# Agent attention and a gated feed-forward on one core: query scores moved one group ahead, score products summed in one PSUM bank

## The chip, the core and the metric

The kernel runs on one core of a Trainium2 chip. The core has a matrix engine (TensorE, PE in the profile; its weight loads are PEld), a vector engine (VectorE, DVE), a scalar engine for activation functions and copies (ScalarE, ACT), GpSimd (POOL) and SyncE (SP), whose queue issues most of the transfers. Each engine works through its own instructions in order and waits for others by semaphores. Matmuls read SBUF and write PSUM; a PSUM tile of this kernel is one bank, 512 float32 per partition.

The metric is the device time of one launch in microseconds; less is better. The kernel before takes 2173.52 us, the median of 3 runs (2172.88 to 2175.33).

## The reference

Four batches of 12480 rows of 128, 49 agents, and a feed-forward of width 2048:

```python
def sm(a, b):
    s = scale * (a @ b.transpose(0, 2, 1))
    s = s - s.max(-1, keepdims=True)
    e = np.exp(s)
    return e / (e.sum(-1, keepdims=True) + 1e-09)
agent_v = sm(agents, k) @ v          # per batch, 49 x 128
x = sm(q, agents) @ agent_v          # per batch, 12480 x 128
h = x @ w_in                         # 49920 x 2048
out = (h * (1.0 / (1.0 + np.exp(-1.702 * h)))) @ w_out
```

The scale is 1/sqrt(128). The weights of the feed-forward come as float64; everything else is float32. q, k and agents are multiplied by 8 after drawing.

## The kernel before

**Layout.** Everything runs transposed, with features on partitions. A group is 960 rows of one batch (`GT`), two halves of 480 (`CH`); a batch has 13 groups, the whole has 52. The hidden width is 16 blocks of 128 (`NF`), so a group has 16 steps and the kernel 832, taken two at a time by `two_steps` (L704): 416 pairs of steps.

**Folded weights.** `agent_v @ w_in` is computed once per batch (`weights_part`, L330, four parts of 512 columns), so that a group's hidden values come from the softmax of the 49 agents instead of from x. Precision is kept by splitting operands into a high half (float32r, a rounded form) and a low half, the rest. For the up matmuls the 49 agent rows and their halves are packed into two tiles `wh` and `wq`, and for each group the softmax is packed into `sa`, `sb` and `rq` (`query_pairs`, L383 to L404): TensorE transposes the softmax (L387), ScalarE casts two high parts (L397), VectorE subtracts the low parts (L399), and eight small transfers on SP's queue (`move`, L345) put rows into their places, the last of them into `rq`.

**A pair of steps.** `up` (L408) runs four matmuls with `sa` or `sb` (L415) and four small ones with `rq` on quarters of the array (L418), into four PSUM tiles, which is all that pool has; four gelus on ScalarE follow (L428). `high` (L431) makes the high half of each gelu tile: by a GpSimd transfer that casts (even steps, L434), on ScalarE (L436, steps 1, 3, 5, 11, 13, 15) or on VectorE (L438, steps 7 and 9). `low` (L441) subtracts on VectorE. `down` (L447) runs six matmuls per step (high by high, low by high, high by low, two halves each) and adds 16 steps up in the two `po` tiles; it works four steps behind (`LAG`). In each pair VectorE takes the low half of the even step two back, and of the odd step just made. TensorE takes the odd step of two first, then the jobs of the second step, then the even one.

**Work beside it.** Lists of jobs per step (`at`, filled by `put`) place the rest by hand. Per group, for the next one: score halves at steps 2 and 3 (`Q_AT`), the shift by the maximum at step 4, exp at 6 (`E_AT`; ScalarE loads another function table for it and then the gelu table again), sums at 8, softmax at 9, transposes and packing at 10 (`P_AT`); for the one after it, the splitting of the loaded queries into three bfloat16 parts at 13 to 16 (`S_AT`, `split`). Per batch, for the next one: 13 key tiles, one each 5 or 6 steps (split, two score halves, partial maximum), the key maximum, then 13 value tiles, two a group (L288), then the four weight parts. `pe_step` keeps TensorE's extra jobs on separate steps.

**Scores.** `scores` (L178) sums six products of bfloat16 parts in four matmuls per block of 120 rows: parts 0 and 1 of the agents side by side (98 columns), part 2 (49 columns), and so on. Each half (four blocks) fills one PSUM tile with two column sets per block; ScalarE copies one set (L193), and VectorE adds the other (L194). The partial maximum of a key tile is a reduction over 8 blocks (L229).

**Order.** The Tile framework sets all semaphores and orders the part ahead of the loop and the first group by its own scheduler; from the second group on the order on TensorE, ScalarE, VectorE and GpSimd is as written (`manual_schedule`, L732). Ahead of the loop lie the loads, the first batch's key scores and values, four conversions of float64 words for `w_in` (`to_float32`, L116, eight VectorE operations), query 0, the four weight parts of batch 0, and one of the four conversions for `w_out`.

Of the kernel before, what the change touches and what calls it, by code (L numbers as in the profile page):

```python
# [42 lines left out]
def kernel(  # L43
# [62 lines left out]
    part_max = const.tile([P, NKG, A], F32, name="part_max")  # L106
# [71 lines left out]
    def scores(b, parts, out, c):  # L178
        x0, x1, x2 = parts
        a = ag_part[:, b].rearrange("p i a -> p (i a)")  # L180
        mm = nc.tensor.matmul
        ps = ps_m.tile([P, 512], F32, name="ps_m")
        for j in range(KB // 2):
            t0 = (c * KB // 2 + j) * TB
            t = slice(t0, t0 + P)
            o = ps[:, j * 2 * A : (j + 1) * 2 * A]
            mm(out=o, lhsT=x0[:, t], rhs=a[:, 0 : 2 * A], start=True, stop=False)  # L187
            mm(out=o[:, A:], lhsT=x0[:, t], rhs=a[:, 2 * A :], start=False, stop=False)
            mm(out=o, lhsT=x1[:, t], rhs=a[:, 0 : 2 * A], start=False, stop=False)  # L189
            mm(out=o[:, 0:A], lhsT=x2[:, t], rhs=a[:, 0:A], start=False, stop=True)  # L190
        s = ps[:TB, : KB * A].rearrange("p (j i a) -> p j i a", i=2, a=A)
        o = out[:, c * KB // 2 : (c + 1) * KB // 2, :]
        nc.scalar.copy(out=o, in_=s[:, :, 0, :])  # L193
        return lambda: nc.vector.tensor_add(out=o, in0=s[:, :, 1, :], in1=o)  # L194
# [7 lines left out]
    def first_key_scores(g, kt):  # L202

        for c in range(2):
# [12 lines left out]
        nc.vector.tensor_reduce(  # L217
            out=part_max[:TB, g, :],
            in_=score[:TB, g * KB : (g + 1) * KB, :].rearrange("p j a -> p a j"),
            axis=AX.X,  # L220
            op=ALU.max,
        )

    def key_scores(b, g, parts, c):
        return scores(b, parts, score[:TB, g * KB : (g + 1) * KB, :], c)

    def key_part_max(g):
        s = score[:TB, g * KB : (g + 1) * KB, :]
        nc.vector.tensor_reduce(  # L229
            out=part_max[:TB, g, :], in_=s.rearrange("p j a -> p a j"), axis=AX.X, op=ALU.max  # L230
        )
# [98 lines left out]
    def weights_part(b, w, c):  # L330
# [23 lines left out]
    def query_scores(n, b, parts, c):  # L354
        sd = e_sb[:TB, :, 0:A]
        return sd, scores(b, parts, sd, c)

    def query_shift(sd):
        m = work.tile([P, KB], F32, name="m")
        nc.vector.tensor_reduce(out=m[:TB], in_=sd, axis=AX.X, op=ALU.max)  # L360
# [70 lines left out]
    def high(f, g):  # L431
        gh = gpool.tile([P, 2, CH], F32R, name="gh", bufs=GH_BUFS)
        if f % 2 == 0:
            nc.gpsimd.dma_start(out=gh, in_=g)  # L434
        elif f in HI_ON_ACT:
            nc.scalar.copy(out=gh, in_=g)  # L436
        else:
            nc.vector.tensor_copy(out=gh, in_=g)  # L438
# [7 lines left out]

    def down(f, gh, gl, po):  # L447
        for lhsT, rhs, first, last in (
# [4 lines left out]
            for c in range(2):  # L453
# [4 lines left out]
                    start=(f == 1 and first),  # L458
                    stop=(f == NF - 2 and last),
# [17 lines left out]
    adds = {}  # L477
# [28 lines left out]
    def do_key_scores(b, g, c):  # L506
        adds[b, g, c] = key_scores(b, g, k_parts[b, g], c)
# [9 lines left out]
    def do_query_scores(n, c):  # L517
        if n < B * NG:
            b, g = divmod(n, NG)
            scored[n], adds[n, c] = query_scores(n, b, q_parts[n], c)  # L520

    def do_query_add(n, c):
        if n < B * NG:
            adds.pop((n, c))()
# [35 lines left out]
    for g in range(NKG):  # L560
# [13 lines left out]
    for c in range(2):  # L574
        do_query_scores(0, c)
        do_query_add(0, c)
    do_query_shift(0)
    do_query_exp(0)
    do_query_sums(0)
    do_query_softmax(0)  # L580
    acc_ps = ps_o.tile([P, 512], F32, name="po0")
    for g in range(NKG):
# [11 lines left out]
        if g in FIRST_UP:  # L594
            up_weights(FIRST_UP.index(g), words_in[FIRST_UP.index(g)])
# [6 lines left out]
    do_query_load(1)  # L602
# [23 lines left out]
    for i in range(1, NF // 4):  # L626
# [147 lines left out]
```

## Time and profile before

| | |
|---|---|
| median of 3 runs | 2173.52 us (2172.88 to 2175.33) |
| the profiled execution | 2182.02 us, span 2180.2 us |
| mean granted TensorE clock | 0.968 |
| busy: PE, DVE, ACT, POOL | 94%, 76%, 67%, 13% of the span |
| first pair of steps | at 78.8 us |
| DMA | 349.46 MB, mean 160 GB/s |

Busy shares are averages over the span. A busy TensorE may run at a lower clock, and matmuls are pipelined, so the distance from one start to the next says what a matmul costs, not its duration. In the lines shown below, an idle time and what ended it stand in brackets or behind the bar. The clock is in parts of full speed.

### The profile page before, as it was taken

How to read it: one execution, taken by the hardware profiler on the slowest of the kernel's cores; microseconds unless marked ns; L12 is line 12 of the kernel's file. 1: busy time of each engine (PE TensorE's matmuls, PEld its weight loads, DVE VectorE, ACT ScalarE, POOL GpSimd, SP SyncE). 2: the span in 40 equal slices, each digit the busy share in tenths (PEclk: the TensorE clock that was granted, in tenths of full speed). 3: DMA queues.
4: the chain of work that ended last, by engine and by line, in shares of the span. 5: the costliest groups of instructions: out<-in, count | busy, mean ns of one | idle time of the engine just before them, and what ended most of it. 6: DMA issues, size and time to landing. Idle time of an engine off the chain costs nothing.

```text
span 2180.2 us, 33873 instructions
## 1 busy us (share of the span) xinstructions
PE 2055.0 (94%) x12232; PEld 1562.0 (72%) x12232; DVE 1659.4 (76%) x2220; ACT 1471.6 (67%) x2602; POOL 287.2 (13%) x577
## 2 busy tenths in 40 slices
PE   7899999999999999999999999999998999999999
PEld 7567776777767777767776777777776777777776
DVE  6699887777779888777777989787676666766665
ACT  3367676676767776676676676666776776767775
POOL 3011111111101111111101111111110111111110
PEclk9799999999999999999999999999999999999999
DMA  9455566686545546777644545776754444443433
GB/s 266 126 175 174 168 161 170 161 188 171 162 134 164 178 153 170 176 179 172 177 145 140 178 153 167 184 168 170 186 137 137 142 136 141 136 142 133 135 133 122
DMA packets 162460, 349.46 MB, mean 160 GB/s; under 512 B 17900, under 2 KB 88332, under 8 KB 162292
## 3 DMA queue, kind: packets, MB, share of 16 engines
q0 software_dynamic: 100464, 223.68, 36.1%
q1 hardware_dynamic: 61828, 123.61, 19.7%
q8 instruction: 96, 1.57, 0.3%
q14 instruction: 72, 0.59, 0.1%
HBM read 100.14 MB, written 25.56 MB: 58 GB/s over the span
## 4 chain that ended last, share of the span: by engine, by line
PE 46%; DMA 17%; issue 10%; DVE 7%; ACT 3%; SPq 3%; POOL 1%; POOLq 0%; ACTq 0%; DVEq 0%
PE po L454 27%; DMA rq<-sb 11%; PE ph L415 8%; PE ph L418 5%; DMA gh<-g 4%; SPq L346 3%; DVE gl L443 3%; ACT g L428 2%; DMA wq<-wl 2%; PE ps_m L290 1%; PE ps_m L187 1%; PE ps_m L387 1%; DVE gh L438 1%; PE ps_m L189 1%; POOL gh L434 1%
## 5 line engine op out<-in xcount | busy, mean ns | idle before, releaser
L428 ACT ACTIVATE g<-ph 128x480 f32<-128x480 f32 x1664 | 821.9, 576 | 596.6 <-PE ph L418 586.6
L443 DVE TENSOR_TENSOR gl<-g,gh 128x960 fp32r<-128x960 f32 x832 | 950.5, 1152 | 241.2 <-DMA gh<-g 122.8
L454 PE MATMUL po<-gh,wo_h 128*128 128x480 f32 x1664 | 564.2, 421 | 0.0
L454 PE MATMUL po<-gl,wo_h 128*128 128x480 f32 x1664 | 512.9, 390 | 0.0
L454 PE MATMUL po<-gh,wo_l 128*128 128x480 f32 x1664 | 510.9, 389 | 0.0
L434 POOL DMA_DIRECT2D gh<-g x416 | 222.5, 535 | 1802.0 <-ACT g L428 1409.5
L454 PEld LDWEIGHTS po<-gl,wo_h 128*128 128x128 f32 x1664 | 322.6, 194 | 53.8 <-issue 0.8
L454 PEld LDWEIGHTS po<-gh,wo_l 128*128 128x128 f32 x1664 | 321.9, 194 | 53.6
L454 PEld LDWEIGHTS po<-gh,wo_h 128*128 128x128 f32 x1664 | 281.5, 194 | 84.9 <-issue 63.5
L415 PE MATMUL ph<-sb,wh 128*128 128x480 f32 x832 | 318.0, 382 | 7.4 <-DMA sb<-sb 7.4
L415 PE MATMUL ph<-sa,wh 128*128 128x480 f32 x832 | 319.2, 384 | 0.5 <-DMA wh<-wl 0.4
L436 ACT CAST gh<-g 128x960 fp32r<-128x960 f32 x312 | 314.3, 1007 | 6.9
L418 PE MATMUL ph<-rq,wq 19*128 19x480 f32 x1664 | 249.4, 483 | 51.2 <-DMA rq<-sb 42.4
L418 PEld LDWEIGHTS ph<-rq,wq 19*128 19x128 f32 x1664 | 97.4, 182 | 216.3 <-issue 140.4
L415 PEld LDWEIGHTS ph<-sb,wh 128*128 128x128 f32 x832 | 157.9, 190 | 35.9 <-issue 9.2
L415 PEld LDWEIGHTS ph<-sa,wh 128*128 128x128 f32 x832 | 158.2, 190 | 28.9 <-issue 2.0
L174 DVE TENSOR_TENSOR rest<-rest 128x488 bf16<-128x488 f32 (+1 forms) x182 | 128.7, 715 | 0.0
L189 PE MATMUL ps_m<-ag_part,rest 128*128 128x98 bf16 x728 | 115.3, 205 | 0.0
L190 PE MATMUL ps_m<-ag_part,rest 128*128 128x49 bf16 x728 | 111.9, 186 | 0.0
L194 DVE TENSOR_TENSOR e_sb<-ps_m,e_sb 120x196 f32<-120x196 f32 x104 | 37.1, 357 | 88.4 <-ACT e_sb L193 88.4
L438 DVE CAST gh<-g 128x960 fp32r<-128x960 f32 x104 | 68.2, 656 | 34.7 <-ACT g L428 34.6
L399 DVE TENSOR_TENSOR sa<-ps_m,sa 49x480 fp32r<-49x480 f32 x52 | 33.9, 651 | 58.9 <-ACT sb L397 54.9
(103 smaller groups left out, 1798.0 us busy)
## 6 DMA issues: line engine op xcount, KB each, us to landing
gh<-g POOLq DMA_DIRECT2D x416, 480.0 KB, 3.8
kt<-kT SPq DMA_DIRECT2D x52, 480.0 KB
qt<-qT SPq DMA_DIRECT2D x52, 480.0 KB
vt<-v SPq DMA_DIRECT2D x52, 480.0 KB
outT<-o SPq DMA_DIRECT2D x104, 240.0 KB
v_pair<-v POOLq DMA_DIRECT2D x39, 480.0 KB, 7.1
rq<-sa SPq DMA_DIRECT2D x104, 35.6 KB
rq<-sb SPq DMA_DIRECT2D x104, 35.6 KB
```

What stands on the lines that cost most here:

```text
L174: nc.vector.tensor_sub(out=halves(r)[1][:, s], in0=r[:, s], in1=halves(r)[0][:, s])
L189: mm(out=o, lhsT=x1[:, t], rhs=a[:, 0 : 2 * A], start=False, stop=False)
L190: mm(out=o[:, 0:A], lhsT=x2[:, t], rhs=a[:, 0:A], start=False, stop=True)
L346: nc.sync.dma_start(out=out.bitcast(F32), in_=in_.bitcast(F32))
L415: nc.tensor.matmul(out=ph[k][:, :CH], lhsT=wh[:, cols[i]], rhs=pairs[c], start=True, stop=False)
L418: nc.tensor.matmul(out=ph[k][:, :CH], lhsT=wq[r, cols[i]], rhs=rq[r], start=False, stop=True, tile_position=(k * 32, 0),)
L428: nc.scalar.activation(out=gs[i][:, c, :], in_=ph[k][:, :CH], func=AF.Gelu_apprx_sigmoid)
L434: nc.gpsimd.dma_start(out=gh, in_=g)
L436: nc.scalar.copy(out=gh, in_=g)
L438: nc.vector.tensor_copy(out=gh, in_=g)
L443: nc.vector.tensor_sub(out=gl, in0=g, in1=gh.bitcast(F32))
L454: nc.tensor.matmul(out=po[c][:, :CH], lhsT=lhsT[:, f, :], rhs=rhs[:, c, :], start=(f == 1 and first), stop=(f == NF - 2 and last),)
```

## The change

- The query work of a group is done two groups ahead up to the shift, and one group ahead from the exp on: splits at steps 8 to 11, score halves at 12 and 13, load and shift at 14, exp at step 0 of the next group, sums and softmax at 2, transposes and packing at 4. Queries 0 and 1 are taken up to the softmax ahead of the loop (`ahead`).
- `scores` runs six matmuls of 49 columns per block, all summed in the same 49 columns; both halves of a tile share one PSUM bank (`score_bank`). ScalarE's copy and VectorE's add of a half go: the query's maximum and shift read the bank, and a key tile is copied once, as a whole (`key_store`).
- The key maximum is kept as a running elementwise maximum over tiles (`running_max`), read from the same bank, and reduced over the 8 blocks at the end.
- High halves: step 1 goes to a GpSimd transfer too, step 3 to VectorE, the other odd steps to ScalarE. Both low halves of a pair are taken in the next pair, the odd one first; that of step 1 one pair later still. The first down matmuls of a group take step 0 first.
- The high half of a value tile is a VectorE copy of the loaded tile in place of a GpSimd transfer. Value matmuls move to steps 6 and 11 of a group (the last tile: 5), key tiles to one each 5.5 steps in batches 1 and 2.
- Ahead of the loop only one `w_in` conversion precedes the value loads; the loads of words alternate between `w_in` and `w_out`. Two weight parts are made ahead of the loop, two in the first group, with their conversions. The first `wq` moves go to GpSimd's queue. The written order holds from the first group on.

```diff
-Q_AT = 2
-E_AT = 6
-P_AT = 10
-S_AT = 13
+Q_AT = 12
+E_AT = 0
+P_AT = 4
+S_AT = 8
 K_AT = 3
-V_AT = 0
-V2_AT = 9
+V_AT = (6, 11)
+V_LAST = 5
-FIRST_WORDS = (1, 3, 5, 7)
-FIRST_UP = (0, 2, 4, 6)
-HI_ON_ACT = (1, 3, 5, 11, 13, 15)
+FIRST_WORDS = 1
+FIRST_UP = 2
+BOTH = (0,)
+ON_DVE = (2,)
...
-    def scores(b, parts, out, c):
+    def scores(b, parts, ps, c):
         x0, x1, x2 = parts
...
+        for j in range(c * KB // 2, (c + 1) * KB // 2):
+            t = slice(j * TB, j * TB + P)
+            o = ps[:, j * A : (j + 1) * A]
+            products = [(x0, 0), (x0, 1), (x0, 2), (x1, 0), (x1, 1), (x2, 0)]
+            for i, (x, y) in enumerate(products):
+                nc.tensor.matmul(
+                    out=o,
+                    lhsT=x[:, t],
+                    rhs=ag_part[:, b, y, :],
+                    start=(i == 0),
+                    stop=(i == len(products) - 1),
+                )
+
+    def score_bank():
         ps = ps_m.tile([P, 512], F32, name="ps_m")
...
+        return ps, ps[:TB, : KB * A].rearrange("p (j a) -> p j a", a=A)
...
+    def running_max(g, s):
+        if g == 0:
+            nc.vector.tensor_copy(out=run_max[:TB], in_=s)
+        else:
+            nc.vector.tensor_tensor(out=run_max[:TB], in0=s, in1=run_max[:TB], op=ALU.max)
+
+    def key_store(g, s):
+        nc.scalar.copy(out=score[:TB, g * KB : (g + 1) * KB, :], in_=s)
+        running_max(g, s)
...
-    def value_hi(b, g):
-        nc.gpsimd.dma_start(out=v_pair[:TB, :, 0:C], in_=v[b, :, g * KB : (g + 1) * KB, :])
-
-    def value_lo(g, vt):
+    def value_pair(vt):
         vp = v_pair
+        nc.vector.tensor_copy(out=vp[:TB, :, 0:C], in_=vt[:TB])
         nc.vector.tensor_sub(out=vp[:TB, :, C : 2 * C], in0=vt[:TB], in1=vp[:TB, :, 0:C].bitcast(F32))
...
-        if f % 2 == 0:
+        if f % 2 == 0 or f - 1 in BOTH:
             nc.gpsimd.dma_start(out=gh, in_=g)
-        elif f in HI_ON_ACT:
+        elif f - 1 in ON_DVE:
+            nc.vector.tensor_copy(out=gh, in_=g)
+        else:
             nc.scalar.copy(out=gh, in_=g)
...
+    def ahead(n):
+        for c in range(2):
+            do_query_scores(n, c)
+        do_query_load(n + 1)
+        do_query_shift(n)
+        do_query_exp(n)
+        do_query_sums(n)
+
+    ahead(0)
     do_query_softmax(0)
...
-    for c in range(F // 512):
+    for c in range(2):
+        if c:
+            up_weights(c, words_in[c])
         weights_part(0, w0, c)
+    for i in range(4):
+        do_query_split(1, i)
+    ahead(1)
+    do_query_softmax(1)
     down_weights(0, words[0])
...
     for i in range(1, NF // 4):
+        if i > 1:
+            put(4 * i - 8, lambda i=i: up_weights(i, words_in[i]))
+            put(pe_step(4 * i - 6), lambda i=i: weights_part(0, w0, i))
         put(4 * i - 3, lambda i=i: down_weights(i, words[i]))
...
-            t = pe_step(s0 + (10 + 5 * k if b == 0 else K_AT + 6 * k))
+            t = pe_step(s0 + (16 + 5 * k if b == 0 else K_AT + 11 * k // 2))
             t1 = pe_step(t + 1)
...
-            put(t1 + 1, lambda b=b, k=k: adds.pop((b + 1, k, 1))())
-            put(t1 + 1, lambda k=k: key_part_max(k))
+            put(t1 + 1, lambda b=b, k=k: do_key_store(b + 1, k))
...
+            t = slot + (V_LAST if last else V_AT[k % 2])
...
+            put(t - 4, lambda b=b, k=k: value_pair(vts.pop((b + 1, k))))
+            put(slot + 3 - last, lambda k=k: key_pair(k))
...
+        if n:
+            put(s0 + E_AT, lambda n=n: do_query_exp(n + 1))
...
+            put(s0 + E_AT + 2, lambda n=n: do_query_sums(n + 1))
+            put(s0 + E_AT + 2, lambda n=n: do_query_softmax(n + 1))
         put(s0 + P_AT, lambda n=n: do_query_pairs(n + 1))
         for i in range(4):
...
+            put(s0 + S_AT + i, lambda n=n, i=i: do_query_split(n + 2, i))
+        for c in range(2):
+            put(s0 + Q_AT + c, lambda n=n, c=c: do_query_scores(n + 2, c))
+        put(s0 + Q_AT + 2, lambda n=n: do_query_load(n + 3))
+        put(s0 + Q_AT + 2, lambda n=n: do_query_shift(n + 2))
...
+        for u in late:
+            do_low(u)
+        late.clear()
         jobs(t)
         if t < steps:
             gh[t] = high(f, g[t])
+            if f not in ON_DVE:
+                gh[t + 1] = high(f + 1, g[t + 1])
         if 2 <= t < steps + 2:
-            gl[t - 2] = low(g.pop(t - 2), gh[t - 2])
-        if t < steps:
+            if (f - 2) % NF in BOTH:
+                late.append(t - 1)
+            else:
+                do_low(t - 1)
+        downs = []
+        if t >= LAG:
+            m, e = divmod(t - LAG, NF)
...
+            downs = [0, 1] if e in BOTH else [1, 0]
+        for k, i in enumerate(downs):
+            u = t - LAG + i
+            down(e + i, gh.pop(u), gl.pop(u), po[m], e + k == 0, e + k == NF - 1)
+            if k == 0:
+                second(t, f)
...
+    def second(t, f):
+        jobs(t + 1)
+        if 2 <= t < steps + 2:
+            do_low(t - 2)
+        if t < steps and f in ON_DVE:
             gh[t + 1] = high(f + 1, g[t + 1])
...
     with tc.manual_schedule(engines={E.PE, E.Activation, E.DVE, E.Pool}):
-        for t in range(NF, steps + LAG, 2):
+        for t in range(0, steps + LAG, 2):
             two_steps(t)
```

More of the change, by code (lines that the diff above doesn't have):

```diff
@@ L105 @@
     score = const.tile([P, NKG * KB, A], F32, name="score")
-    part_max = const.tile([P, NKG, A], F32, name="part_max")
+    run_max = const.tile([P, KB, A], F32, name="run_max")
     max_b = const.tile([P, A], F32, name="max_b")
@@ L216, in first_key_scores @@
             nc.scalar.copy(out=score[:TB, i * KB // 2 : (i + 1) * KB // 2, :], in_=s)
[L217 to L231, printed above, removed]
+        running_max(g, score[:TB, g * KB : (g + 1) * KB, :])
+    def running_max(g, s):
[6 more added lines that the diff above has]
+        running_max(g, s)
     def key_max_0(d):
         mx = work.tile([P, A], F32, name="mx", bufs=1)
-        nc.vector.tensor_reduce(
-            out=mx[:TB], in_=part_max[:TB].rearrange("p g a -> p a g"), axis=AX.X, op=ALU.max
-        )
+        nc.vector.tensor_reduce(out=mx[:TB], in_=run_max[:TB].rearrange("p j a -> p a j"), axis=AX.X, op=ALU.max)
         d["mx"] = mx
@@ L342, in weights_part, with move @@
         for i in range(4):
-            move(wq[i * 32 : i * 32 + A - R, s], wl[R:A])
-    def move(out, in_):
-        nc.sync.dma_start(out=out.bitcast(F32), in_=in_.bitcast(F32))
+            move(wq[i * 32 : i * 32 + A - R, s], wl[R:A], None if b or c else nc.gpsimd)
+    def move(out, in_, queue=None):
+        (queue or nc.sync).dma_start(out=out.bitcast(F32), in_=in_.bitcast(F32))
     def query_load(b, g):
@@ L352, in query_load, with query_shift @@
         return t
-    def query_scores(n, b, parts, c):
+    def query_shift(s):
+        m = work.tile([P, KB], F32, name="m")
+        nc.vector.tensor_reduce(out=m[:TB], in_=s, axis=AX.X, op=ALU.max)
         sd = e_sb[:TB, :, 0:A]
[L356 to L360, printed above, removed]
         nc.vector.tensor_tensor(
-            out=sd, in0=sd, in1=m[:TB].unsqueeze(2).broadcast_to([TB, KB, A]), op=ALU.subtract
+            out=sd, in0=s, in1=m[:TB].unsqueeze(2).broadcast_to([TB, KB, A]), op=ALU.subtract
         )
+        return sd
     def query_exp(e):
@@ L444, in low, with down @@
         return gl
-    def down(f, gh, gl, po):
+    def down(f, gh, gl, po, begin, end):
         for lhsT, rhs, first, last in (
@@ L457, in down @@
                     rhs=rhs[:, c, :],
-                    start=(f == 1 and first),
-                    stop=(f == NF - 2 and last),
+                    start=(begin and first),
+                    stop=(end and last),
                 )
@@ L476 @@
     scored = {}
-    adds = {}
+    banks = {}
     sums = {}
@@ L506, in do_key_scores, with do_key_store @@
     def do_key_scores(b, g, c):
-        adds[b, g, c] = key_scores(b, g, k_parts[b, g], c)
+        if c == 0:
+            banks[b, g] = score_bank()
+        scores(b, k_parts[b, g], banks[b, g][0], c)
+    def do_key_store(b, g):
+        key_store(g, banks.pop((b, g))[1])
     def do_key_values(b, g):
@@ L518, in do_query_scores @@
         if n < B * NG:
[L519 to L524, printed above, removed]
+            if c == 0:
+                banks[n] = score_bank()
+            scores(n // NG, q_parts[n], banks[n][0], c)
     def do_query_shift(n):
         if n < B * NG:
-            query_shift(scored[n])
+            scored[n] = query_shift(banks.pop(n)[1])
     def do_query_exp(n):
@@ L565 @@
         nc.sync.dma_start(out=vt0[:TB, g % 2, :, 0:C], in_=v[0, :, g * KB : (g + 1) * KB, :])
-        if g in FIRST_WORDS:
-            words_in.append(load_words(w_in, len(words_in)))
-    words = [load_words(w_out, i) for i in range(NF // 4)]
+        if g == FIRST_WORDS:
+            words_in.append(load_words(w_in, 0))
+    words = []
+    for i in range(NF // 4):
+        if i:
+            words_in.append(load_words(w_in, i))
+        words.append(load_words(w_out, i))
     for g in range(NKG):
@@ L573 @@
     key_max()
[L574 to L579, printed above, removed]
+    def ahead(n):
[6 more added lines that the diff above has]
+    ahead(0)
     do_query_softmax(0)
@@ L626 @@
     for i in range(1, NF // 4):
+        if i > 1:
+            put(4 * i - 8, lambda i=i: up_weights(i, words_in[i]))
+            put(pe_step(4 * i - 6), lambda i=i: weights_part(0, w0, i))
         put(4 * i - 3, lambda i=i: down_weights(i, words[i]))
-    for i in range(4):
-        put(0, lambda i=i: do_query_split(1, i))
     exps = {}
@@ L702, in jobs @@
             job()
+    late = []
     def two_steps(t):
```

72 lines of the change are left out of this document (17 added, 55 removed).

## The prediction

> **What bounds the kernel now.** I read the page's busy shares, then the lines of the pair's first matmul, then TensorE's timeline around the start of a group, then who waits, then the granted clock by stretch.
>
> ```profile
> PE 2055.0 (94%) x12232; PEld 1562.0 (72%) x12232; DVE 1659.4 (76%) x2220; ACT 1471.6 (67%) x2602; POOL 287.2 (13%) x577
> ```
> ```profile
> L415 PE MATMUL ph<-sa,wh x832: 374/380/769, 78.8 to 2167.1; 128*128 128x480 f32 x167
> ```
> ```profile
> 1004.90 0.38 PE L415 MATMUL ph<-sa,wh 128*128 128x480 f32 x1
> ...
> 1009.01 0.38 PE L415 MATMUL ph<-sa,wh 128*128 128x480 f32 x1
> ...
> 1012.03 1.20 PE L290 MATMUL ps_m<-v_pair,e_pair 120*128 120x258 f32 x8
> ...
> 1014.37 0.39 PE L415 MATMUL ph<-sa,wh 128*128 128x480 f32 x1
> ```
>
> TensorE (PE) sets the time, but its 94% includes waiting. L415 runs `sa` twice in a pair of steps, so 832 matmuls are 416 pairs, and the last pair starts at 2167.1 - 0.4 = 2166.7. A pair that waits for nothing takes 1009.01 - 1004.90 = 4.11 us (4.10 below); the average is (2166.7 - 78.8)/415 = 5.03. A value tile adds 5.36 - 4.10 = 1.26. Now the first pair of a group, and the score tile in the pair after it:
>
> ```profile
> 1872.19 0.38 PE L415 MATMUL ph<-sa,wh 128*128 128x480 f32 x1
> ...
> 1874.91 0.48 PE L418 MATMUL ph<-rq,wq 19*128 19x480 f32 x1 [0.95 <-DMA rq<-sb]
> ...
> 1878.04 0.38 PE L415 MATMUL ph<-sa,wh 128*128 128x480 f32 x1
> ...
> 1879.43 0.22 PE L187 MATMUL ps_m<-ag_part,qt 128*128 128x98 bf16 x1
> 1879.49 0.19 PE L188 MATMUL ps_m<-ag_part,qt 128*128 128x49 bf16 x1
> 1879.52 0.20 PE L189 MATMUL ps_m<-ag_part,rest 128*128 128x98 bf16 x1
> 1879.56 0.19 PE L190 MATMUL ps_m<-ag_part,rest 128*128 128x49 bf16 x1
> ...
> 1880.01 0.46 PE L454 MATMUL po<-gh,wo_h 128*128 128x480 f32 x1
> ```
> ```profile
>   DMA rq<-sb: 110.7, 123
> ```
> ```profile
> 1860.93 0.60 PE ps_m L387 x4
> ...
> 1868.66 6.21 DMA rq<-sb
> ```
> ```profile
> 1833.90:1837.30 3.40, 2.47 (x11) 1.39 (x9) 3.35 (x4) 2.19 (x4) 0.26 (x1) 1.00 0.48 165
> 1837.40:1840.80 3.40, 3.40 (x9) 2.86 (x10) 2.23 (x2) 1.57 (x2) 0.17 (x1) 0.53 0.41 147
> ```
>
> That first pair took 5.85 us: its last L418 matmul waited for the transfer `rq<-sb`. The chain says why: transposed at 1860.93 (step 10 of the group before), the pieces are moved in one queue, and the last transfer lands 6.21 us after its issue, at 1874.87, 14 us in all, where step 10 leaves six steps, or 12.3 us. This wait sums to 110.7 us over 123 waits (list for tile `rq`). The windows' rows give length, busy time of PE, PEld, DVE, ACT and POOL, granted clock, DMA share and GB/s: one group's first pair left TensorE idle for 0.93 of 3.40 us, and in the next 3.40 us the clock stood at 0.53. Some stalls are paid again in slow matmuls.
>
> In clean terms the stretch from 78.8 to 2166.7 is 415 x 4.10 = 1702; 90 score tiles of two halves, 1880.01 - 1879.43 = 0.58 each, 1.2 with the switch: 108; 39 value tiles: 49; 51 transposes at about 0.5: 26; weight parts 12, from 24 of these 32 matmuls:
>
> ```profile
> L336 PE MATMUL ps_m<-w_in_sb,avT 128*128 128x512 f32 x32 | 18.9, 689 | 2.6 <-DVE avT L324 2.4 <-DVE wl L339 0.2
> ```
>
> That is 1897 of 2088. TensorE loses 191 us, 111 of it directly to `rq`.
>
> **The change, part by part.** *Queries ahead.* Transposes and moves go from step 10 to step 4: twelve steps, 24.6 us at least, for the chain of 14. SP's queue carries the same eight moves, now ahead of the loads of the later steps and behind the stores of step 2; the first weight parts' `wq` moves go to GpSimd's queue, which is idle then. The `rq` stall goes from every group but the first. What is late next is the Vector engine's low half of step 3, as below.
>
> *Scores.* Four matmuls per block (98, 49, 98, 49 columns) become six of 49. The rows give 0.06 and 0.04 after a 98-column matmul and 0.03 after a 49-column one; 16 in 0.58 us are 36 ns on average, about 43 and 27, each with its own weight load. Six at 27 are 162 ns against 140: +0.18 us a tile. Bounds: 24 ns each would make it +0.03, 43 ns (a load that does not keep up) +0.94. I take 27, since 49-column matmuls with weight loads are in the rows. The Trainium skill (TensorE: Matmul & The Clock Gate, Back-to-back issue gap) speaks against the change: a stream of weight load and matmul pairs sustains about 81 ns even at 128 columns; by it, as an estimate, 16 more a tile cost 1.3 us, 115 us in all. The trace disagrees: 36 ns on average, and the measurement decides.
>
> *Vector and Scalar work.*
>
> ```profile
> L193 ACT COPY e_sb<-ps_m 120x196 f32<-120x196 f32 x104 | 37.3, 358 | 10.1 <-PE ps_m L190 10.1
> L194 DVE TENSOR_TENSOR e_sb<-ps_m,e_sb 120x196 f32<-120x196 f32 x104 | 37.1, 357 | 88.4 <-ACT e_sb L193 88.4
> L194 DVE TENSOR_TENSOR score<-ps_m,score 120x196 f32<-120x196 f32 x78 | 28.0, 359 | 5.8 <-ACT score L193 5.2
> L229 DVE TENSOR_REDUCE part_max<-score 120x49 f32<-120x392 f32 x39 | 33.2, 851 | 1.3
> L269 DVE TENSOR_TENSOR score<-score,max_b 120x392 f32<-120x392 f32 x40 | 23.1, 578 | 0.0
> L438 DVE CAST gh<-g 128x960 fp32r<-128x960 f32 x104 | 68.2, 656 | 34.7 <-ACT g L428 34.6
> ```
>
> Vector loses both adds (37 + 28), half of L438's casts (34), and 39 x (0.851 - 0.578) = 11 by the running maximum at L269's price; it gains the values' high half, 1024 columns at about L438's 0.66 to 0.7, 39 times: 27. Net -83, to 1576 us, 76% of the new span; Scalar loses about 40. Neither is the bound over a group. Their order is: these engines work in order, and Vector work waiting for Scalar holds the low halves behind it, which TensorE's down matmuls need. Three places:
>
> (1) Step 0, exp. Two table loads and an exp now follow the group's first pair.
>
> ```profile
> 1854.52 1.28 ACT L366 ACT_TABLE_LOAD   x1
> 1855.81 0.53 ACT L366 ACTIVATE e_sb<-e_sb 120x392 f32<-120x392 f32 x1
> 1856.36 1.28 ACT L428 ACT_TABLE_LOAD   x1
> 1857.65 1.96 ACT L428 ACTIVATE g<-ph 128x480 f32<-128x480 f32 x4
> ```
>
> A pair's gelus end 1.39 + 0.1 + 1.96 = 3.45 after its start (1.39, the up matmuls, is 1879.43 - 1878.04), so the exp ends at 3.45 + 1.28 + 0.53 = 5.3 and gelu resumes 1857.65 - 1854.52 = 3.13 later, at 6.6. The next pair's gelus then end at 8.5, and its successor (8.2) wants its fourth PSUM tile at 8.9: no stall. A key exp of two tiles adds 0.7 (twice the columns of the 0.53 row, in one instruction): at most 0.4. On Vector the sums and softmax follow the exp, 1.3 at L269's price, then with keys four pair copies, 1.9 less some overlap; the value pair fits into the gap ahead of the exp. `low` of step 0 (1.15, half of the 2.23 row below) then ends at 7.8, with keys at 9.7, for a down matmul at 8.2 + 1.39 + 0.5 = 10.1: hidden by 0.4 to 2.3.
>
> (2) Step 4, the pairs.
>
> ```profile
> 1859.27 0.38 PE L415 MATMUL ph<-sa,wh 128*128 128x480 f32 x1
> ...
> 1863.99 0.38 PE L415 MATMUL ph<-sa,wh 128*128 128x480 f32 x1
> ```
> ```profile
> 1863.75 0.65 DVE L399 TENSOR_TENSOR sa<-ps_m,sa 49x480 fp32r<-49x480 f32 x1 [1.90 <-ACT sb L397]
> 1864.43 0.66 DVE L399 TENSOR_TENSOR sb<-ps_m,sb 49x480 fp32r<-49x480 f32 x1
> 1865.12 2.23 DVE L443 TENSOR_TENSOR gl<-g,gh 128x960 fp32r<-128x960 f32 x2
> ```
>
> Vector's subtractions wait behind Scalar's gelus and casts; the first `low` after them ends at 1865.12 + 1.15 = 1866.27. In the changed order the next pair's first down matmul, at 1863.99 + 1.39 = 1865.38, needs just that `low` (step 3): 0.95 us stall, in groups without values. In value groups the key-value matmuls (1.26) stand ahead of it at step 6 and hide it; I leave 0.3.
>
> (3) Key tiles. The maximum now reads the PSUM bank in the same step as Scalar's copy of it. The 1863.75 row shows such a reader waiting for the other engine's last read of its bank: `sa`'s subtraction needs the `sa` cast and waits for `sb`'s. On an even step the copy comes after the pair's matmuls and four gelus (1.39 + 1.96) and takes about 0.5 (0.36 for half of it at L193), so it ends at 4.0, the maximum at 4.5, two split pieces 1.2, `low` 1.1: 5.7 to 6.9, for a down matmul at 4.10 + 1.39 = 5.5. That is 0.2 to 1.4 for about half the stores and something like it when it cascades: 1.9 us a group of three.
>
> *High halves and lag.* Step 1 goes to a GpSimd transfer as well, and every `low` is now taken a pair after its high half. `low` of odd steps no longer waits for its cast; nothing is charged. Each g buffer is held longer, and with five of them gelu stalls about when TensorE would anyway. The value transfers on GpSimd's queue go.
>
> *Start.*
>
> ```profile
> 78.80:126.10 47.30, 43.54 (x194) 27.19 (x195) 34.83 (x57) 28.58 (x49) 4.43 (x11) 0.78 0.42 135
> 126.10:173.10 47.00, 43.77 (x335) 33.66 (x334) 43.14 (x64) 31.05 (x59) 5.23 (x13) 0.96 0.51 165
> ```
> ```profile
> 65.07 0.43 DVE L124 TENSOR_SCALAR tmp<-words 128x512 uint32<-128x512 uint32 x1 [3.34 <-DMA words<-w_out]
> ...
> 68.07 0.28 DVE L600 COPY acc<-po 49x128 f32<-49x128 f32 x1
> ...
> 68.35 0.67 DVE L136 SCALAR_TENSOR_TENSOR m<-m,tmp 128x512 f32<-128x512 f32 x1
> ```
>
> The first two groups took 94 us, at clocks of 0.78 and 0.96. The accumulator copy waited at 68.07 behind a conversion; two weight parts instead of four precede the loop, but query 1's scores and softmax (5 us of Vector work) come in. First pair at 77 (70 to 84). In group 0 Vector has five conversions (two up, three down), 68.35 + 0.67 - 65.07 = 3.9 with the copies in between, 3.6 each, 18; 16 lows at 1.1, 17.6; the rest about 8: 43 against TensorE's 36: 7 lost, and 2 in group 1.
>
> *Sum.* 77 + 416 x 4.10 (1706) + 89 score tiles at 1.38 (123) + values 49 + transposes 26 + weights 14 + tail after the last pair 2180.2 - 2166.7 - 4.1 = 9.4: 2004. Stalls: start 9; 18.5 plain groups at 0.95: 18; 19.5 value groups: 6; 13 key groups: 25; batch changes 3: 61. Slow clock: before, 191 less 111 and some 50 of other waits leaves about 30, 0.2 a stalled microsecond: 12. (The Trainium skill, TensorE: Matmul & The Clock Gate, What's actually happening, has the clock fall only after an idle window of about 3.4 us; by it the short stalls here would cost no clock, and the time would be 12 less. The trace disagrees: TensorE was busy 2.47 of the 3.40 us before the 0.53.) Together 2077 of span, 2079 for the profiled run (2182.02 against its span 2180.2). The median of the runs is 2173.52, 0.996 of the profiled one: **2071**.
>
> **Rivals.** *Vector's waits reach TensorE.* Price a wait on Scalar by L194's, 88.4/39 = 2.3 us. Three per group, exp, pairs and key stores or value pairs, 6.8 us, would be 347 over 51 groups if all reached the down matmuls: 2004 + 9 + 347 of span, 2353 by the median. It is slower than before once half of it arrives (2186 - 2013 = 173). Against it: the Vector engine's slack of 4.1 - 2.2 a pair, and that it waits like this now (88.4 at L194 alone) with little stall from it. Slower: 0.07. A quarter to 40% arriving, 87 to 139 in place of the 61 + 12, gives 2094 to 2145: 0.18.
>
> *Scores at 43 ns:* a weight load that does not keep up with six small matmuls, 89 x 0.76 = +68, 2138: 0.04. For it speaks only that six such in a row, into one region, are not in the trace. (The skill's rule on weight load and matmul pairs points this way.)
>
> *`rq` still late:* were the moves held in SP's queue behind loads, the stall would stay and the scores add 16: with the steadier start about 2175, the same: 0.03.
>
> *All hidden:* no stall but the start's, 2004 + 9 + 2, 2007 by the median, up to 2040: 0.10.
>
> **How the numbers follow.** The forecast, 2045 to 2095, has 0.58. The range 2030 to 2130 leaves out most of the hidden case, the 43 ns case and the slower one. A measurement of this kernel tells about 0.2% (4 us) from no change: faster 0.90, same 0.03, slower 0.07.
>
> **What would show it.** `rq` gone from TensorE's waits; the first pair of a group at 4.1 to 4.3; 48 score matmuls per tile 27 ns apart; no wait of Vector on a score copy in the query's path, but waits on Scalar at the key maximum; the pair after step 4 at about 5.0 in groups without values; clock near 0.99. It is wrong if plain groups take over 37 us (35.6 forecast: 32.8 + 1.38 + 0.5 + 0.95), or if down matmuls wait for `gl` by more than 2 us a group.

## The result and the profile after

The changed kernel takes 2052.34 us (median of 4, 2051.60 to 2052.63); beside it on the same chip the kernel before took 2174.43. The ratio is 0.9429 (95%: 0.9399 to 0.9458): 122 us less, where 102 were forecast. The profiled execution took 2051.6 us with a span of 2049.8, 27 less than the 2077 of the sum.

First the page's busy shares, then the up matmul's line (its first start and its last), then what TensorE's matmuls, its weight loads (PEld) and Vector waited for (us in total, times, longest):

```profile
PE 1998.1 (97%) x13688; PEld 1522.0 (74%) x13688; DVE 1575.9 (77%) x2025; ACT 1443.7 (70%) x2457; POOL 280.1 (14%) x594
```
```profile
L407 PE MATMUL ph<-sa,wh x832: 372/381/769, 77.0 to 2036.5; 128*128 128x480 f32 x167
```
```profile
PE po L445 <- DVE gl L435: 14.3, 17, 5.0
PE ph L410 <- DMA wq<-wl: 6.7, 7, 2.2
```
```profile
PEld po L445 <- DVE gl L435: 36.3, 59, 5.4
PEld ph L407 <- ACT g L420: 21.1, 69, 2.8
```
```profile
DVE sa L391 <- ACT sb L389: 81.8, 42, 7.2
DVE run_max L225 <- ACT score L228: 81.2, 33, 6.9
```

`rq` is gone from TensorE's waits, where it stood with 110.7 us. TensorE executes 1456 more instructions and is busy for 57 us less. Vector's busy time came out as summed: 1575.9 against 1576. Vector waits for Scalar at these two lines for 163 us in all; before, the waits at the score add and at `sa` came to 88.4 + 54.9 = 143.3. The down matmuls and their weight loads wait for low halves (`gl`) for 14.3 + 36.3 = 50.6 us, about 1 us a group. The first pair starts at 77.0. From the starts of L407's rows, the first pairs of all groups together fell from 378.8 to 219.8 us (52 of them), a plain group takes 35.3 us, and a clean pair still takes 4.10. The mean granted clock is 0.988, up from 0.968.

The fourth pair of a plain group stalls, by these rows of a late group's timeline (start, duration, engine, line, operation; the wait before it in brackets):

```profile
1773.88 0.65 DVE L391 TENSOR_TENSOR sa<-ps_m,sa 49x480 fp32r<-49x480 f32 x1 [2.38 <-ACT sb L389]
1773.90 0.38 PE L407 MATMUL ph<-sa,wh 128*128 128x480 f32 x1
...
1774.56 0.66 DVE L391 TENSOR_TENSOR sb<-ps_m,sb 49x480 fp32r<-49x480 f32 x1
...
1775.25 4.36 DVE L435 TENSOR_TENSOR gl<-g,gh 128x960 fp32r<-128x960 f32 x4
...
1776.47 0.71 PE L445 MATMUL po<-gl,wo_h 128*128 128x480 f32 x2 [0.47 <-DVE gl L435]
...
1778.77 0.38 PE L407 MATMUL ph<-sa,wh 128*128 128x480 f32 x1
```

The pair takes 1778.77 - 1773.90 = 4.87 us: Vector idles 2.38 us for Scalar's casts, subtracts twice, and only then makes the low half for which the down matmul waits.

In a group with value tiles another pair stalls too, the third: it takes 5.07 us in most of these 18 groups, against 4.47 in a plain one. Scalar's rows at the start of one:

```profile
1401.37 1.28 ACT L358 ACT_TABLE_LOAD   x1
...
1403.10 0.84 ACT L269 ACTIVATE score<-score 120x784 f32<-120x784 f32 x1
...
1405.25 1.96 ACT L420 ACTIVATE g<-ph 128x480 f32<-128x480 f32 x4
```

The exp of two key tiles (L269) stands beside the query's exp, gelu stands still for 1405.25 - 1401.37 = 3.88 us, and three up matmuls of the third pair wait for a gelu to free their PSUM tile. That is most of the 21.1 us in the list above.

The half score tile of the next step, between its first matmul and the down matmul behind it:

```profile
1788.37 0.25 PE L186 MATMUL ps_m<-ag_part,qt 128*128 128x49 bf16 x3
...
1789.00 0.68 PE L445 MATMUL po<-gh,wo_h 128*128 128x480 f32 x2
```

24 matmuls in 0.63 us are 26 ns each. The Trainium skill (TensorE: Matmul & The Clock Gate, Back-to-back issue gap) has about 81 ns for a sustained pair of weight load and matmul at 128 columns, and an issue floor of about 25 ns for one matmul of up to 64 columns. The trace agrees with the second, though each of these matmuls has its own weight load. A whole tile costs 5.43 - 4.10 = 1.33 us.

Two groups stand out, the first (51.8 us) and the fourteenth, the first of the second batch (52.7 us where its like take 39). The first, as the view of windows has it (length; busy PE, PEld, DVE, ACT, POOL; granted clock; DMA share; GB/s):

```profile
76.98:128.81 51.83, 42.22 (x192) 27.92 (x193) 46.07 (x74) 26.67 (x47) 5.06 (x11) 0.77 0.51 164
```

### The profile page after: what moved, and what is told of

Its sections match the earlier page's. It is cut to its first block, busy times and chain, and to the rows that moved or that the text cites. A ratio compares the mean times of both kernels' runs of the same rounds, so it can differ in the third digit from the quotient of the medians.

```text
span 2049.8 us, 36357 instructions
## 1 busy us (share of the span) xinstructions
PE 1998.1 (97%) x13688; PEld 1522.0 (74%) x13688; DVE 1575.9 (77%) x2025; ACT 1443.7 (70%) x2457; POOL 280.1 (14%) x594
## 4 chain that ended last, share of the span: by engine, by line
PE 78%; DVE 8%; DMA 4%; issue 4%; ACT 4%; SPq 1%; POOL 1%; ACTq 0%; DVEq 0%; POOLq 0%
PE po L445 46%; PE ph L407 15%; PE ph L410 7%; PE ps_m L186 5%; DVE gl L435 4%; ACT g L420 2%; DMA wq<-wl 2%; PE ps_m L284 2%; PE ps_m L209 1%; DVE sb L391 1%; SPq L340 1%; DMA outT<-o 1%; DVE rest L175 1%; DVE rest L173 1%; POOL score L265 1%
## 5 line engine op out<-in xcount | busy, mean ns | idle before, releaser
L445 PE MATMUL po<-gh,wo_h 128*128 128x480 f32 x1664 | 551.2, 412 | 0.0
L445 PE MATMUL po<-gl,wo_h 128*128 128x480 f32 x1664 | 504.1, 384 | 16.1 <-DVE gl L435 14.3
L445 PE MATMUL po<-gh,wo_l 128*128 128x480 f32 x1664 | 499.9, 382 | 0.0
L426 POOL DMA_DIRECT2D gh<-g x468 | 250.1, 534 | 1702.8 <-ACT g L420 1154.6
L445 PEld LDWEIGHTS po<-gl,wo_h 128*128 128x128 f32 x1664 | 309.0, 189 | 82.9 <-DVE gl L435 36.3
L407 PE MATMUL ph<-sa,wh 128*128 128x480 f32 x832 | 320.3, 385 | 4.1 <-DMA wh<-wl 2.2
L407 PE MATMUL ph<-sb,wh 128*128 128x480 f32 x832 | 322.1, 387 | 0.0
L410 PE MATMUL ph<-rq,wq 19*128 19x480 f32 x1664 | 208.9, 483 | 6.7 <-DMA wq<-wl 6.7
L410 PEld LDWEIGHTS ph<-rq,wq 19*128 19x128 f32 x1664 | 81.4, 182 | 145.9 <-issue 136.6
L407 PEld LDWEIGHTS ph<-sa,wh 128*128 128x128 f32 x832 | 157.6, 189 | 36.9 <-ACT g L420 9.6
L407 PEld LDWEIGHTS ph<-sb,wh 128*128 128x128 f32 x832 | 157.5, 189 | 35.4 <-ACT g L420 11.5
L186 PE MATMUL ps_m<-ag_part,rest 128*128 128x49 bf16 x2184 | 128.2, 185 | 0.0
L186 PEld LDWEIGHTS <-rest 128*128 128x128 bf16 x2184 | 108.6, 97 | 0.1
L225 DVE TENSOR_TENSOR run_max<-ps_m,run_max 120x392 f32<-120x392 f32 x36 | 20.4, 566 | 81.3 <-ACT score L228 81.2
L186 PEld LDWEIGHTS <-qt 128*128 128x128 bf16 x1248 | 61.7, 98 | 25.5 <-issue 25.4
```

Of the source, the lines that this page charges most:

```text
L186: nc.tensor.matmul(out=o, lhsT=x[:, t], rhs=ag_part[:, b, y, :], start=(i == 0), stop=(i == len(products) - 1),)
L407: nc.tensor.matmul(out=ph[k][:, :CH], lhsT=wh[:, cols[i]], rhs=pairs[c], start=True, stop=False)
L410: nc.tensor.matmul(out=ph[k][:, :CH], lhsT=wq[r, cols[i]], rhs=rq[r], start=False, stop=True, tile_position=(k * 32, 0),)
L445: nc.tensor.matmul(out=po[c][:, :CH], lhsT=lhsT[:, f, :], rhs=rhs[:, c, :], start=(begin and first), stop=(end and last),)
```

## The experiments

The theory: the gain is the lead of the queries, since the 14 us from the transposes to the landed `rq` now have room. The rival: the gain is the lighter Vector and Scalar work and its order. Times are medians; ratios are to the kernel before on the same chip.

**The packing put back to step 10.**

```diff
-P_AT = 4
-S_AT = 8
+P_AT = 10
+S_AT = 5
```

> The changed kernel with the transposes and packing put back to step 10 of the group before use (splits at 5 so that the written order fits); everything else stays changed. Theory, the lead: the chain from transposes to the landed rq takes 14 us and six steps are 12.3 us, so rq is late again at nearly every group; the direct waits were 111 us before and some 20 us of slow clock came with them: 2150 to 2185 us, first pair of a group at 5.5 to 7.5 us, rq back in TensorE's waits with some 100 us. Rival, the lighter Vector and Scalar engines (score bank, running maximum, order of the halves) brought the gain: 2047 to 2060 us, no rq in the waits.

Measured 2097.9 us, ratio 0.9635 (0.9611 to 0.966): 46 us over the changed kernel, between the two ranges: less than expected but far from none. One group's transposes and the next group's first pair, and the list of waits:

```profile
1824.27 0.63 PE L379 MATMUL ps_m<-ident,p_pad 120*128 120x120 f32 x4
```
```profile
1837.02 0.38 PE L407 MATMUL ph<-sa,wh 128*128 128x480 f32 x1
...
1839.13 0.47 PE L410 MATMUL ph<-rq,wq 19*128 19x480 f32 x1 [0.66 <-DMA rq<-sb]
...
1842.25 0.39 PE L407 MATMUL ph<-sa,wh 128*128 128x480 f32 x1
```
```profile
PE ph L410 <- DMA rq<-sb: 18.0, 22, 1.9
```

`rq` is late again, and the first pair takes 5.23 us. The first pairs of 51 groups take 266.3 us in place of 215.6: 51 us more, a little over the whole difference. The size was off because the lead is not the same six steps as before: now the scores stand in it, at 12 and 13, so that 1837.02 - 1824.27 = 12.75 us pass from the transposes to the group, where before it was 1872.19 - 1860.93 = 11.26. The lead theory stands; the expectation forgot what lies inside the lead.

**The packing at step 8.** The same edit with `P_AT = 8`.

> The same with the transposes at step 8 (splits at 5 too): eight steps are 16.4 us. Theory, the lead with a threshold at 14 us: no wait for rq, 2046 to 2058 us, as with step 4 within 0.3%. If instead each step of lead brought a share of the gain (queues that are only shifted), a third of the way from step 4 to 10 would be lost here twice over: 2090 to 2140 us.

Measured 2108.66 us, ratio 0.9687 (0.9661 to 0.9712). A miss. `rq` was in time:

```profile
PE po L445 <- DVE gl L435: 52.5, 50, 5.0
...
PE ph L410 <- DMA rq<-sb: 3.7, 2, 2.2
```
```profile
1830.76 0.65 DVE L391 TENSOR_TENSOR sa<-ps_m,sa 49x480 fp32r<-49x480 f32 x1 [4.58 <-ACT sb L389]
...
1832.10 0.72 DVE L175 TENSOR_TENSOR rest<-rest 128x480 bf16<-128x480 f32 x1
...
1833.90 0.70 PE L445 MATMUL po<-gl,wo_h 128*128 128x480 f32 x2 [1.05 <-DVE gl L435]
```

The loss is the changed kernel's own stall, made larger: behind the subtractions Vector has a split piece too, and the pair takes 5.42 us. At step 10 the scores of step 12, ahead of that down matmul, hid all but 0.12 us of it; at step 8 nothing does.

**The packing at step 8, with the low half first.** To test that reading, the edit of the run "The low half first" below was added to it, here for the low half of step 7.

> The kernel with transposes at step 8 (splits at 5), with the low half of step 7 ahead of the pairs' subtractions. Theory: that kernel's loss against the changed one (57 us, though rq was in time) is the down matmuls of the next pair waiting for that low half (sixth pair 5.42 us); it falls to 4.1 to 4.5 and the time to 2049 to 2074 us. Rival: the loss comes from the splits, three steps earlier, in front of other low halves: 2095 to 2110 us.

Measured 2059.32 us, ratio 0.9449 (0.9422 to 0.9475): 49 us back, and that pair takes 4.14. So the lead at step 8 is enough for `rq`, and what the earlier run lost was the low half's place in Vector's queue.

**The lead alone, in the kernel before.**

```diff
-Q_AT = 2
-E_AT = 6
-P_AT = 10
-S_AT = 13
+Q_AT = 12
+E_AT = 0
+P_AT = 4
+S_AT = 8
...
-V_AT = 0
-V2_AT = 9
+V_AT = 10
+V2_AT = 3
```

Queries 0 and 1 go ahead of the loop as in the change; both value tiles of a pair stand in one group, and key tiles come at 8 + 5k and 3 + 5.5k.

> The kernel before with the queries' lead alone: queries 0 and 1 ahead of the loop, scores at 12 and 13, exp at 0, packing at 4; scores, partial maximum, halves, value transfers and conversions as before (key tiles and value matmuls moved a little, to fit in front of the end of a batch). Theory, the lead: the 111 us of rq and about 20 us of slow clock go, a part comes back as waits of Vector behind Scalar: 2050 to 2085 us. Rival, the lighter engines: 2165 to 2180 us. If the lead only works together with the bank (Vector's adds wait for Scalar's copies in the way): 2100 to 2150 us.

Measured 2078.82 us, ratio 0.9547 (0.9523 to 0.9571): the lead alone brings 98 us of the change's 122, so the rival does not carry the gain. Its first group takes 63.3 us, against 47.3 before and 51.8 in the changed kernel; from the second group to the last pair the lead alone saves 115 us and the whole change 133. The rival is not worth nothing: the run with the old scores, below, has the lead and the same form of scores as this one, with all the other edits, and is 2078.82 - 2038.0 = 41 us faster, 9 of it in the first group. No run tells these other edits apart.

The third pair of a plain group takes 5.70 us here, 4.47 in the changed kernel. I put that down to the softmax at step 3.

**The lead alone, softmax at step 2.**

```diff
-            put(s0 + E_AT + 3, lambda n=n: do_query_softmax(n + 1))
+            put(s0 + E_AT + 2, lambda n=n: do_query_softmax(n + 1))
```

> The kernel before with the lead alone, and the softmax one step earlier (2, as in the changed kernel). Theory: in the lead-alone kernel the third pair of a group takes 5.70 us against 4.47 in the changed one because the transposes at step 4 wait for a softmax taken at step 3 behind low halves; it falls by up to 1.2 us a group: 2017 to 2045 us, so that lead and softmax together bring the whole gain. Rival: the wait is for Scalar's exp and the order of the low halves, and little changes: 2065 to 2080 us.

Measured 2074.09 us, ratio 0.9522 (0.9494 to 0.955): that reading falls, the pair takes 5.70 still. Scalar's rows at the start of a group, here and then in the changed kernel, show another:

```profile
1783.11 1.28 ACT L366 ACT_TABLE_LOAD   x1
1784.40 0.53 ACT L366 ACTIVATE e_sb<-e_sb 120x392 f32<-120x392 f32 x1
1784.84 0.98 ACT L436 CAST gh<-g 128x960 fp32r<-128x960 f32 x1
1785.83 1.28 ACT L428 ACT_TABLE_LOAD   x1
1787.13 1.96 ACT L428 ACTIVATE g<-ph 128x480 f32<-128x480 f32 x4
```
```profile
1764.64 1.28 ACT L358 ACT_TABLE_LOAD   x1
1765.94 0.53 ACT L358 ACTIVATE e_sb<-e_sb 120x392 f32<-120x392 f32 x1
1766.49 1.28 ACT L420 ACT_TABLE_LOAD   x1
1767.78 1.96 ACT L420 ACTIVATE g<-ph 128x480 f32<-128x480 f32 x4
```

With the old halves Scalar casts the high half of step 1 between the exp and the next gelus: gelu stands still for 1787.13 - 1783.11 = 4.02 us instead of 3.14. TensorE's weight loads in the third pair of the first of these kernels show who pays:

```profile
1788.21 0.19 PEld L415 LDWEIGHTS ph<-sb,wh 128*128 128x128 f32 x1 [0.28 <-ACT g L428]
1788.67 0.19 PEld L415 LDWEIGHTS ph<-sa,wh 128*128 128x128 f32 x1 [0.28 <-ACT g L428]
1789.14 0.19 PEld L415 LDWEIGHTS ph<-sb,wh 128*128 128x128 f32 x1 [0.28 <-ACT g L428]
...
1790.62 0.19 PEld L454 LDWEIGHTS po<-gh,wo_h 128*128 128x128 f32 x1 [0.25 <-ACT o L465]
1791.08 0.19 PEld L454 LDWEIGHTS po<-gh,wo_h 128*128 128x128 f32 x1 [0.27 <-ACT o L465]
```

Three up matmuls wait for a gelu to free their PSUM tile, and the group's first down matmuls for Scalar's copy of the last group's output: 1.36 us. The change gives the cast to a GpSimd transfer (`BOTH`). So the exp at step 0 needs the new halves to be free; this is read from the traces and was not run by itself. The Trainium skill (ScalarE: Activation LUTs, What ACT_TABLE_LOAD costs) gives 1.28 us for the load, as here, and 1.38 for a drain with each switch; these rows leave 0.05 us between them, so no drain shows here.

**The old scores in the changed kernel.** Four matmuls per block, two halves, Scalar's copy and Vector's add, as in the kernel before; the running maximum reads SBUF.

```diff
-                put(t1 + 1, lambda b=b, k=k: do_key_store(b + 1, k))
+                put(t + 1, lambda b=b, k=k: do_add(b + 1, k, 0))
+                put(t1 + 1, lambda b=b, k=k: do_add(b + 1, k, 1))
+                put(t1 + 1, lambda b=b, k=k: do_key_store(b + 1, k))
...
+            put(s0 + Q_AT + c + 1, lambda n=n, c=c: do_add(n + 2, c))
```

> The changed kernel with the old scores: four matmuls per block, two halves, Scalar copies one column set and Vector adds the other; the running maximum then reads SBUF. Theory, the bank is no part of the gain: TensorE saves 89 x (1.33 - 1.24) = 8 us, Vector gets 65 us of adds back but has slack of 470 us: 2040 to 2062 us. Rival, the bank's saving on Vector and its waits is what counts: the adds wait for Scalar by 2 us each as before, and those that reach TensorE add 40 to 100 us: 2090 to 2150 us.

Measured 2038.0 us, ratio 0.9362 (0.9339 to 0.9384): 14 us faster than the changed kernel, and 2 below the expected range. Vector's adds wait again, and the time does not show it:

```profile
DVE e_sb L195 <- ACT e_sb L194: 49.1, 40, 5.7
```

Vector is 59 us busier (1635.0), and it does not matter. The score tile costs 5.36 - 4.10 = 1.26 (89 tiles: 6 us), and key groups lose about 0.6 us less each. The one-bank score, part of the change, cost time.

**The running maximum later.**

```diff
         nc.scalar.copy(out=score[:TB, g * KB : (g + 1) * KB, :], in_=s)
-        running_max(g, s)
...
+            put(t1 + 2, lambda k=k: running_max(k, score[:TB, k * KB : (k + 1) * KB, :]))
```

> The changed kernel with the running maximum one step later and from the copied tile in SBUF, so that Vector does not wait for Scalar's copy of the bank (81.2 us of waits, 33 times). Theory after the old-scores run: about 0.5 us of each key group reached TensorE, 7 us in all: 2042 to 2048 us. The recorded forecast's price, 1.9 us a key group: 25 us less, 2023 to 2030 us. All hidden: 2049 to 2055 us.

Measured 2045.19 us, ratio 0.9389 (0.9365 to 0.9412): 7 us less, about the other half of the 14. The two ratios' intervals overlap, but the slowest run here, 2048.87, lies under the fastest of the changed kernel, 2051.60, and by the starts of the groups 7 us come from key groups and 3 from the fourteenth. Of the 81.2 us, 45.0 remain, since Vector now needs the copy itself; so 36 us of waits less saved 7 of time. The wait at the bank is the case of which the Trainium skill speaks (PSUM — Partial Sum Buffer, PSUM bank collisions raise a hardware error): the compiler's scheduler adds a dependency between instructions of different engines on the same bank and quadrant of partitions, reads and writes alike. The trace agrees: Vector's read of the bank waited for Scalar's, 33 times.

**The low half first.**

```diff
         late.clear()
+        if f == P_AT and 2 <= t < steps + 2:
+            do_low(t - 1)
         jobs(t)
...
-            else:
+            elif f != P_AT:
```

> The changed kernel with one move: in the pair that transposes the next softmax (step 4), Vector takes the low half of step 3 ahead of the two subtractions of the pairs. Theory: the fourth pair of a group, 4.87 us in plain groups against 4.10, waits for just that low half, which is queued behind subtractions that wait for Scalar's casts; it falls to 4.1 and the time by 0.75 x 18 to 0.75 x 25: 2033 to 2040 us. Rival: the wait only moves to the next low half in Vector's queue (step 2), which the subtractions now delay: 2048 to 2056 us.

Measured 2035.62 us, ratio 0.9342 (0.9319 to 0.9365). The same place as in the changed kernel's fourth pair:

```profile
1765.75 0.65 DVE L391 TENSOR_TENSOR sa<-ps_m,sa 49x480 fp32r<-49x480 f32 x1 [1.31 <-ACT sb L389]
...
1767.71 0.60 PE L445 MATMUL po<-gl,wo_h 128*128 128x480 f32 x2
```

Vector waits 1.31 instead of 2.38 us, the down matmul waits for nothing, and the pair takes 4.14. The stall of step (2) of the prediction is shown, with its price, 17 us.

**The wq moves of the second batch on GpSimd's queue.**

```diff
-            move(wq[i * 32 : i * 32 + A - R, s], wl[R:A], None if b or c else nc.gpsimd)
+            move(wq[i * 32 : i * 32 + A - R, s], wl[R:A], nc.gpsimd if b == 1 or b + c == 0 else None)
```

> The changed kernel with the wq moves of the second batch's weights on GpSimd's queue (as those of the first part already are). Theory: the first group of the second batch took 52.7 us against 39 because these moves stand in SP's queue behind the moves of the pairs, which wait for Vector; it falls to 40 to 43 us and the time by 10 to 13: 2039 to 2043 us. Rival: the weights are late anyway, made too close to their use: 2048 to 2056 us. Cost: 16 more transfers on GpSimd ahead of high halves, up to 3 us.

Measured 2043.41 us, ratio 0.9378 (0.9355 to 0.9402); the fourteenth group takes 43.6 us instead of 52.7. In the changed kernel (Vector's subtraction, SP's queue, TensorE):

```profile
605.23 0.68 DVE L333 TENSOR_TENSOR wl<-ps_m,wh 49x512 fp32r<-49x512 f32 x1 [0.71 <-ACT wh L331]
```
```profile
607.14 2.31 SPq L340 DMA_DIRECT2D sb<-sb  x2
609.50 1.24 SPq L340 DMA_DIRECT2D rq<-sb  x2
610.84 1.68 SPq L340 DMA_DIRECT2D wh<-wl  x2
612.57 2.46 SPq L340 DMA_DIRECT2D wq<-wl  x4
```
```profile
625.31 0.49 PE L410 MATMUL ph<-rq,wq 19*128 19x480 f32 x1 [2.17 <-DMA wq<-wl]
```

The last part was ready at 605.9 and its `wq` moves were issued from 612.57 on, behind the pairs' moves.

**The first group.** Two edits: the cast of `w_out`'s high half on Vector, and the five conversions in the loop cut to one operation each.

```diff
-        nc.scalar.copy(out=wo_h[:, s, :], in_=wo)
+        nc.vector.tensor_copy(out=wo_h[:, s, :], in_=wo)
```

> The changed kernel with the high half of the converted w_out cast on Vector in place of Scalar. Theory: in the first group Scalar's cast waits for Vector's conversion and the gelus of a pair are queued behind it (TensorE idle around 100 us from the start); without it the first group falls from 51.8 to 43 to 47 us: 2042 to 2048 us. Rival: the first group is bound by Vector's five conversions, and the cast, added to Vector, costs 4 x 0.4 us: 2051 to 2056 us.

Measured 2054.28 us, ratio 0.9427 (0.9404 to 0.945), first group 53.8 us. The theory falls.

```diff
+        if in_loop:
+            o = out if out is not None else work.tile([P, 512], F32, name="m21", tag="o")
+            ts(out=o, in0=hi.bitcast(F32), scalar1=2.0**-6, scalar2=None, op0=ALU.mult)
+            return o
```

> The changed kernel with the five conversions of float64 words in the first group cut to one Vector operation each (seven of eight left out, so the weights' values are others). Theory: the first group (51.8 us) is bound by Vector, 5 x 3.4 us of conversions; it falls to 38 to 42 us: 2038 to 2043 us. Rival: it is bound by the chain of weight parts, moves and gelus or by a slow clock after the idle start: 46 us or more, 2047 to 2053 us.

Measured 2054.6 us, ratio 0.9425 (0.939 to 0.9461), first group 51.3 us. This theory falls too. In the changed kernel Scalar's cast waits for the conversion and the gelus and low halves come behind it; with short conversions that wait is gone, and a weight part's transfer is the late one. Rows of the changed kernel, then of the run:

```profile
102.70 0.62 ACT L146 CAST wo_h<-m 128x512 fp32r<-128x512 f32 x1 [9.12 <-DVE m L137]
103.34 1.96 ACT L420 ACTIVATE g<-ph 128x480 f32<-128x480 f32 x4
...
105.16 1.17 PE L445 MATMUL po<-gl,wo_h 128*128 128x480 f32 x2 [4.97 <-DVE gl L435]
```
```profile
103.50 1.68 SPq L346 DMA_DIRECT2D wh<-wl  x2
...
112.35 0.74 PE L413 MATMUL ph<-sa,wh 128*128 128x480 f32 x1 [3.09 <-DMA wh<-wl]
```

So it seems that two chains of about the same length end in the first group, Vector's conversions and the weight parts' moves in SP's queue. Shorter conversions alone do not make it shorter; the moves alone, and both together, were not tried.

**The three gains together:** old scores, low half first, `wq` moves on GpSimd's queue.

> The changed kernel with the old scores, the low half of step 3 ahead of the pairs' subtractions, and the second batch's wq moves on GpSimd's queue. If the three gains are apart from each other: 2052 - 14 - 17 - 9 = 2012 us (2008 to 2016). If the old scores' Vector work takes back what the earlier low half gives: 2020 to 2030 us.

Measured 2014.52 us (2013.96 to 2016.17), ratio 0.9243 (0.9218 to 0.9269): the gains nearly add up, 38 us under the changed kernel where 14 + 17 + 9 = 40. Plain groups take 34.5 us, the fourteenth 41.1.

## Why the prediction was right, point by point

- **What bound the kernel: `rq`'s lateness.** Right, and shown from both sides: the lead alone brings 98 us, and taking it back lets `rq` be late again for 46. The six steps were priced at 12.3 us; by the rows from the transposes to the group they were 11.26.
- **First pair, clean pair, Vector's sum.** 77 and 77.0; 4.10 and 4.10; 1576 and 1575.9.
- **Score tiles.** 1.38 forecast, 1.33 measured, against 1.26 for the old form: the 27 ns a matmul were right, and the other price that stood beside them, 1.3 us a tile, was not, with 0.07 measured. What I did not price is that the trade itself loses: Vector's saved work was worth nothing, and the bank that two engines read cost 7 us.
- **Value tiles.** Mis-sized: 1.26 forecast, 5.05 - 4.10 = 0.95 measured, 39 x 0.31 = 12 us. The 5.36 of before that I called clean held a wait of its own; the shortest of its kind there was 5.08.
- **The stall after step 4.** 0.95 x 18.5 = 18 us forecast; 4.87 - 4.10 = 0.77 us in a plain group, and 17 us by the run that removes it, 9 of them in the 12 groups that have no other work than the query's. I had counted 18.5 such groups. In value groups it is hidden, as argued: their fourth pair takes 5.09, a value tile over a clean one.
- **Key groups.** Mis-sized: 25 us forecast; all that these groups lose comes to 12, and 7 us came back with 36 of the 81.2 us of waits. Vector did wait for the copy, but I let the wait arrive at TensorE on half the stores. Rival one, Vector's waits reaching TensorE, is answered by the same numbers: of 163 us of them at two lines, the runs that shorten these waits bring back 17 + 7.
- **The exp at step 0.** Right in plain groups: gelu resumes 3.14 us later (3.13 forecast) and the wait hides. It does not hide in value groups, where the key exp adds to it: 3.88 us, and 0.6 us a group on the third pair, where I had allowed 0.4 at most. What seems to carry the plain groups is an edit that I charged with nothing, step 1's cast on GpSimd: with the cast on Scalar the third pair took 1.2 us more, though no run moves that cast alone.
- **Start and batch changes.** Both too small: the first group took 51.8 us, 43 forecast, and the batch changes were given 3 us where the first of them alone cost 9 by the run that mends most of it. The failed step is that of SP's queue: I counted the pairs' moves against loads and stores, and not the weight parts' moves behind the pairs' moves.
- **Together.** The span came out 27 under the sum. Taking 4.10 a pair and the measured price of each tile off the lengths of the groups leaves what each kind lost: 16 us in the first group (9 forecast for the start), 10 in the 12 plain groups (18), 14 in the 18 value groups (6), 12 in the 14 key groups (25), and 18 in the six groups at batch changes (3), of which the fourteenth has 12. Slow clock, a term of 12, is within these figures: from 128.81 to 2036.00 the mean granted clock was 1.00. That makes 70 in place of 73, close only because the misses cancel. The rest, 25, is clean work priced too high: values 12, transposes at 0.37 for 0.5 us 6, score tiles 4, weight parts 2. So the total looks better than its parts, and that is luck.

## What to carry to other kernels

When a packed operand goes through a DMA queue, count the chain from its first instruction to its last landing, and what lies inside the lead, before moving anything else. In an in-order engine, put the work that the bounding engine needs next ahead of work that waits for a third engine; that alone was worth 17 to 49 us here. Saving work on an engine with slack was worth nothing here, and the saving cost time by the matmuls that it added to the engine that bounds.

## What the runs showed that I had not expected

- The same stall after the packing costs 0.1 to 1.3 us a group, by which job TensorE has between it and the down matmul: all but 0.12 hidden at step 10 behind scores, 0.77 at step 4, 1.3 at step 8.
- 98-column and 49-column matmuls in turn (16 a half tile) and 49-column ones alone (24) differ by only 0.07 us a tile, though the second has half as many instructions again: 26 ns each against 36 on average.
- In the first group the granted clock was 0.77 on average while TensorE was busy 42.22 of 51.83 us; part of that busy time is slow matmuls (one of L407 took 0.60 us at 106.93, against 0.38).
